# Hardware loops on VectorE and ScalarE in a decode kernel that streams its cache

## The chip, the cores and the metric

The kernel runs on one core of a Trainium2 chip. The metric is the device time of one execution in microseconds (us). A ratio is the mean time of one kernel's runs over the mean of the other's runs of the same rounds, so it is not quite the ratio of the medians that are quoted beside it.

## The reference

One decode step of a block with adaptive layer norm, for 8 sequences of one token each. The attention has 32 query heads over 8 cached key and value heads of 8192 positions and 128 columns each, in bf16. All else is small.

```python
mod = (_silu(c) @ w_mod).reshape(8, 6, 1, -1)
sa, ca, ga, sb, cb, gb = ...                       # six rows of mod
h = _layernorm(x) * (1 + ca) + sa
q = (h @ wq) ...                                   # 8 x 32 heads x 128
scores = einsum('bhqd,bhkd->bhqk', q, k) * 128 ** -0.5
o = einsum('bhqk,bhkd->bhqd', _softmax(scores), v)
x = x + ga * (o @ wo)
h = _layernorm(x) * (1 + cb) + sb
x = x + gb * (relu(h @ w1 + b1) ** 2 @ w2 + b2)
```

Keys and values together are 268 MB. Every byte of them is read once.

## The kernel before

A ring of four slots of 4 MB in SBUF holds "units". A unit is two heads' keys or values of one sequence (called a batch in the code). A batch has four key units and four value units. SyncE issues all loads in order, and each load waits until its slot is released.

The key part of a batch transposes every key tile on TensorE (`key_tiles`). VectorE and ScalarE copy the transposed tiles out of PSUM, and TensorE forms scores. Then come the maximum, the exponentials, and the transposes of the probabilities. In the value part TensorE multiplies each value unit by the probabilities, VectorE copies the sum (`O_sb`), and four small "gather" matmuls bring it into place.

```python
def load(n):                                   # unit n goes to slot n % 4
    ...
    dep = [released.get(s)]
    loaded[n] = dma("sync", s_ring[s], lambda e: e.dma_start(slot(s), src), dep)
...
for b in range(B):
    Pg.at = (b, "a")
    k_Qb = op("vector", lambda e, b=b: e.tensor_copy(Qb[:], QTm[:, b, :, :]), [k_QTm], "vecP")
    for p in range(NP):                        # four key units
        for k in range(4):
            t, toks = key_tiles(n, k, qn % 2)
            if k == 3:
                released[n % NSLOT] = t        # the last key transpose frees the slot
                load(n + NSLOT)
            if pend is not None:
                maxes.append(scores(b, *pend))
    ...                                        # maximum, exponentials
    for k in range(4):
        for i in range(8):
            for hf in range(2):                # two column halves in turn
                t = op("tensor", ... is_transpose=True, tile_position=(0, 64 * hf)) ...
    ...
    for p in range(NP):                        # four value units
        for m in range(32):
            t = op("tensor", ...)              # probabilities times values
        released[n % NSLOT] = t                # the last of them frees the slot
        load(n + NSLOT)
        t = op("vector", ... tensor_copy(osb, Obank) ...)
        for i in range(4):
            t = op("tensor", ... SEL ...)      # the gather
        ... op("vector", ... tensor_tensor(oTn ...))
```

```python
def _tensor(self, eng, passes):
    ...
    with nc.Fori(0, passes, engines=[pe], head_slot={pe: 0}) as i:
        for j, o in enumerate(part((0, "a"))):
            self._emit(eng, o, first["a", j], seen)
        with eng.If(i < passes - 1):
            ...                                # part "b": the values
            self._emit(eng, None, self.per, seen)
            eng.drain()
            for s, n in self.per.items():
                eng.sem_inc(s, -n)
```

## Time and profile before

| | before |
|---|---|
| time, median of 4 | 670.87 us (670.69 to 670.91) |
| read from HBM | 283.66 MB, 424 GB/s over the span |
| data queue's share of 16 DMA engines | 99.0% |
| busy: TensorE, VectorE, ScalarE | 75%, 45%, 35% |

These lines are from the page of the kernel before. The first gives the busy time of the engines in a span of 669.0 us. The DMA and GB/s rows show 40 equal slices, a digit of 9 meaning busy 90% or more. Then come two DMA queues (packets, MB, share of 16 engines): q1 carries the data, q14 instructions. The last two lines give loads by source (count, KB each, median us from issue to landing).

```profile
PE 499.3 (75%) x7348; PEld 340.7 (51%) x7348; DVE 300.2 (45%) x570; ACT 236.1 (35%) x282; POOL 17.5 (3%) x71
...
DMA  9999999999999999999999999999999999999996
GB/s 375 434 405 437 415 435 433 432 427 433 433 437 428 427 437 431 433 429 431 435 435 428 427 433 437 427 429 433 435 437 428 423 435 439 429 427 433 435 410 250
...
q1 hardware_dynamic: 12900, 283.65, 99.0%
...
q14 instruction: 10, 0.07, 0.0%
...
ring<-in_A_k_cache_dram SPq DMA_DIRECT2D x32, 4096.0 KB, 35.1
ring<-in_A_v_cache_dram SPq DMA_DIRECT2D x31, 4096.0 KB, 28.3
```

The DMA is at least 90% busy in every slice but the last. Key loads land 35.1 us (median) after their issue, though one 4 MB unit takes only about 9.7 us (4096 KB at 432 GB/s). So several units are queued at a time. Loads are issued long before their turn.

The windows view of one batch of the kernel before has, per stretch, the length, each engine's busy time with its count, TensorE's granted clock, the DMA share and GB/s. The first stretch is keys and softmax, the second values.

```profile
core 0: us, PE busy (x) PEld busy (x) DVE busy (x) ACT busy (x) POOL busy (x), PEclk, DMA share, GB/s
431.85:480.30 48.45, 47.22 (x726) 35.45 (x727) 32.63 (x57) 28.54 (x34) 0.00 (x0) 0.97 1.00 432
480.30:509.60 29.30, 11.77 (x145) 4.47 (x146) 3.65 (x9) 0.00 (x0) 0.00 (x0) 0.78 1.00 432
```

The stream runs at 432 GB/s in both, although the engines do quite different work in them.

The timeline of the kernel before, around the same batch's turnover, has start, duration, engine, line, operation, tiles, count, and in brackets the idle time before and who ended it.

```profile
474.87 0.69 ACT L533 ACTIVATE P_sb<-PS,negm 128x512 bf16<-128x512 f32 x1 [2.52 <-DVE negm L529]
...
475.70 2.64 PE L542 MATMUL PS<-IDENT,P_sb 128*64 128x128 bf16 x64 [0.15 <-ACT P_sb L533]
...
476.38 2.56 DVE L555 COPY Pm<-PS 64x512 bf16<-64x512 bf16 x6 [1.54 <-PE PS L542]
...
480.29 1.91 PE L583 MATMUL PS<-ring,Pm 128*32 128x512 bf16 x32
482.24 21.60 SPq L344 DMA_DIRECT2D ring<-in_A_k_cache_dram  x4
...
482.99 0.26 PE L596 MATMUL PS<-SEL,O_sb 128*128 128x8 bf16 x4 [0.80 <-DVE O_sb L592]
...
504.64 0.22 DVE L506 COPY Qb<-QTm 128x256 bf16<-128x256 bf16 x1
...
509.58 2.63 PE L451 MATMUL PS<-IDENT,ring 128*128 128x128 bf16 x23 [5.05 <-DMA ring<-in_A_k_cache_dram]
510.65 0.69 DVE L458 COPY KTb<-PS 128x1024 bf16<-128x1024 bf16 x1 [5.79 <-PE PS L451]
511.50 1.02 ACT L456 ACTIVATE KTb<-PS 128x1024 bf16<-128x1024 bf16 x1 [32.52 <-PE PS L451]
```

The last three lines (TensorE, VectorE, ScalarE) show how long the engines wait between batches: TensorE 5.05 us for the DMA, VectorE 5.79 us, ScalarE 32.52 us. The SPq line needs care: it merges four key-load issues, and 21.60 us runs from the start of the first to the end of the last. In narrow windows the trace shows that each takes 0.33 us. The first starts at 482.24, the others are these:

```profile
485.13 0.33 SPq L344 DMA_DIRECT2D ring<-in_A_k_cache_dram  x1
...
493.57 0.33 SPq L344 DMA_DIRECT2D ring<-in_A_k_cache_dram  x1
...
503.51 0.33 SPq L344 DMA_DIRECT2D ring<-in_A_k_cache_dram  x1
```

The value matmuls of the four units end at 482.20, 485.09, 493.52 and 503.46. So each load is issued within 0.05 us of the release of its slot, and none of the four is held up by the DMA. What is queued ahead of a load can be told from the landings in the trace: at 482.24 two value units are outstanding and land at 490.10 and 499.82, 17.6 us later. This is the tightest point of the batch.

### The profile page before, as it was taken

The numbers are of one execution on the slowest core, as the hardware profiler recorded it, in microseconds if no ns is written. First come the engines' busy times: TensorE is split into PE (matmuls) and PEld (weight loads), VectorE is DVE, ScalarE is ACT, GpSimd is POOL, SyncE is SP. The second block draws the span as 40 slices with busy tenths as digits, with TensorE's granted clock in tenths as the row PEclk, the third lists the DMA queues.
The fourth block names the chain that finished last, engine by engine and source line by source line (L and its number), as shares of the span: only waits on it lengthen the run. The fifth ranks groups of instructions, "written<-read, shape, count | busy, mean of one in ns | idle before, by whom it ended". The sixth has DMA issues, their size and how long they took to land.

```text
span 669.0 us, 15914 instructions
## 1 busy us (share of the span) xinstructions
PE 499.3 (75%) x7348; PEld 340.7 (51%) x7348; DVE 300.2 (45%) x570; ACT 236.1 (35%) x282; POOL 17.5 (3%) x71
## 2 busy tenths in 40 slices
PE   3494964899539984699748995399836995489976
PEld 2383731676228751577317751287414772177634
DVE  1262741467216661367315671167513673156722
ACT  2051630466005640266204650066402652046600
POOL 7200000000000000000000000000000000000000
PEclk9696996799859995599968997699977999779985
DMA  9999999999999999999999999999999999999996
GB/s 375 434 405 437 415 435 433 432 427 433 433 437 428 427 437 431 433 429 431 435 435 428 427 433 437 427 429 433 435 437 428 423 435 439 429 427 433 435 410 250
DMA packets 12969, 283.93 MB, mean 424 GB/s; under 512 B 1267, under 2 KB 2324, under 8 KB 4373
## 3 DMA queue, kind: packets, MB, share of 16 engines
q1 hardware_dynamic: 12900, 283.65, 99.0%
q8 instruction: 11, 0.18, 0.1%
q14 instruction: 10, 0.07, 0.0%
q10 hardware_dynamic: 48, 0.02, 0.0%
HBM read 283.66 MB, written 0.01 MB: 424 GB/s over the span
## 4 chain that ended last, share of the span: by engine, by line
PE 50%; DMA 39%; DVE 5%; ACT 2%; SPq 2%; issue 1%
DMA ring<-in_A_k_cache_dram 37%; PE PS L451 36%; PE PS L466 9%; DVE Pm L555 3%; PE PS L583 2%; DMA ring<-in_B_w_dram 2%; SPq L624 2%; ACT KTb L456 1%; ACT P_sb L533 1%; DVE m L471 1%; PE PS L542 1%; PE PS L442 1%; PE PS L562 0%; DVE rhs_r L559 0%; DVE Dm L524 0%
## 5 line engine op out<-in xcount | busy, mean ns | idle before, releaser
L456 ACT ACTIVATE KTb<-PS 128x1024 bf16<-128x1024 bf16 x192 | 196.5, 1024 | 360.2 <-PE PS L451 360.2
L451 PE MATMUL PS<-IDENT,ring 128*128 128x128 bf16 x4096 | 267.6, 228 | 50.7 <-DMA ring<-in_A_k_cache_dram 50.7
L451 PEld LDWEIGHTS PS<-IDENT,ring 128*128 128x128 bf16 x4096 | 246.9, 102 | 99.4 <-DMA ring<-in_A_k_cache_dram 54.0
L458 DVE COPY KTb<-PS 128x1024 bf16<-128x1024 bf16 x320 | 210.1, 687 | 151.1 <-PE PS L451 148.8
L583 PE MATMUL PS<-ring,Pm 128*32 128x512 bf16 x992 | 82.5, 492 | 63.9 <-DMA ring<-in_A_v_cache_dram 63.0
L592 DVE CAST O_sb<-PS 128x512 bf16<-128x512 f32 x31 | 21.4, 692 | 144.5 <-PE PS L583 144.5
L466 PE MATMUL PS<-KTb,Qb 128*32 128x512 bf16 x1024 | 79.2, 386 | 4.5 <-ACT KTb L456 4.5
L583 PEld LDWEIGHTS PS<-ring,Pm 128*32 128x32 bf16 x992 | 29.5, 116 | 102.3 <-DMA ring<-in_A_v_cache_dram 64.4
L442 PE MATMUL PS<-IDENT 128*128 128x512 bf16 x120 | 31.3, 380 | 0.0
L533 ACT ACTIVATE P_sb<-PS,negm 128x512 bf16<-128x512 f32 x32 | 21.5, 685 | 18.9 <-DVE negm L529 18.9
L596 PEld LDWEIGHTS PS<-SEL,O_sb 128*128 128x128 bf16 x124 | 5.3, 99 | 44.8 <-DVE O_sb L592 44.8
L596 PE MATMUL PS<-SEL,O_sb 128*128 128x8 bf16 x124 | 8.0, 171 | 24.8 <-DVE O_sb L592 24.8
L466 PEld LDWEIGHTS PS<-KTb,Qb 128*32 128x32 bf16 x1024 | 15.5, 94 | 21.1 <-ACT KTb L456 8.5
L555 DVE COPY Pm<-PS 64x512 bf16<-64x512 bf16 x48 | 19.5, 419 | 13.4 <-PE PS L542 12.4
L471 DVE TENSOR_REDUCE m<-PS 128x1 f32<-128x512 f32 x32 | 22.0, 689 | 6.6 <-PE PS L466 6.6
L542 PE MATMUL PS<-IDENT,P_sb 128*64 128x128 bf16 x512 | 20.4, 222 | 2.0 <-ACT P_sb L533 1.1
L542 PEld LDWEIGHTS PS<-IDENT,P_sb 128*64 128x64 bf16 x512 | 15.2, 109 | 9.8 <-ACT P_sb L533 9.8
L442 PEld LDWEIGHTS PS<-IDENT 128*128 128x128 bf16 x120 | 9.9, 103 | 10.8 <-issue 3.4
L599 DVE TENSOR_TENSOR oTn<-PS,rinv 128x8 bf16<-128x8 f32 x31 | 6.0, 194 | 10.9 <-PE PS L596 10.9
L377 PE MATMUL PS<-ring,KTb 128*32 128x512 bf16 x56 | 7.2, 627 | 3.7 <-DMA ring<-in_A_wq_dram 3.7
L552 ACT ACTIVATE Pm<-PS 64x512 bf16<-64x512 bf16 x16 | 9.5, 592 | 1.1
L690 ACT ACTIVATE std<-PS,epst 128x8 f32<-128x8 f32 x1 | 0.3, 267 | 25.0 <-PE PS L689 25.0
(126 smaller groups left out, 101.8 us busy)
## 6 DMA issues: line engine op xcount, KB each, us to landing
ring<-in_A_k_cache_dram SPq DMA_DIRECT2D x32, 4096.0 KB, 35.1
ring<-in_A_v_cache_dram SPq DMA_DIRECT2D x31, 4096.0 KB, 28.3
ring<-in_A_wq_dram SPq DMA_DIRECT2D x1, 4096.0 KB, 20.3
ring<-in_w_mod_dram SPq DMA_DIRECT2D x1, 3072.0 KB, 10.4
wo_sb<-in_A_wo_dram SPq DMA_DIRECT2D x1, 3072.0 KB, 45.5
ring<-in_A_v_cache_dram SPq DMA_DIRECT2D x1, 2048.0 KB, 23.4
ring<-in_B_w_dram SPq DMA_DIRECT2D x3, 512.0 KB, 17.6
ring<-in_B_w_dram SPq DMA_DIRECT2D x1, 1344.0 KB, 20.9
```

What stands on the lines that cost most here:

```text
L442: op("tensor", lambda e: e.matmul(bank(at).rearrange("p (a r) -> p a r", a=4), IDENT[:, :], rhs))
L451: t = op("tensor", lambda e, j=j, i=i: e.matmul(STG[j][:, i, :], src[:, 32 * k + 8 * j + i, :], IDENT[:, :], is_transpose=True), [loaded[n ...
L456: stg_free[j] = op("scalar", lambda e, j=j, dst=dst: e.activation(dst, STG[j], ACT.Copy), [t], "scaP")
L458: stg_free[j] = op("vector", lambda e, j=j, dst=dst: e.tensor_copy(dst, STG[j]), [t], "vecP")
L466: t = op("tensor", lambda e, hf=hf, q=q, rhs=rhs: e.matmul(PS[32 * q:32 * (q + 1), k, :], Qb[:, 2 * p + hf, :], rhs, start=(p == 0 and hf ...
L471: return op("vector", lambda e: e.tensor_reduce(m4[:, k:k + 1], bank(k), AX.X, ALU.max), [t])
L533: exps.append(op("scalar", lambda e, k=k: e.activation(P_sb[:, k, :], bank(k), ACT.Exp, bias=negm[:, 0:1], scale=inv_sqrt, accum_out=rs4[: ...
L542: t = op("tensor", lambda e, k=k, i=i, hf=hf, src=src: e.matmul(STG[k][64 * hf:64 * (hf + 1), i, :], src, IDENT[:, :], is_transpose=True, ...
L555: done.append(op("vector", lambda e, dst=dst, frm=frm: e.tensor_copy(dst, frm), [t, k_pm], "vecP"))
L583: t = op("tensor", lambda e, p=p, m=m, cg=cg, vt=vt, Obank=Obank: e.matmul(Obank[32 * cg:32 * (cg + 1), :], lhs[:, p, 32 * m:32 * m + 32], ...
L592: t = op("vector", lambda e, osb=osb, Obank=Obank: e.tensor_copy(osb, Obank), [t], "vecP")
L624: d_w2 = [dma("sync", s_w2[i], lambda e, a=a, z=z, j=j: e.dma_start(W2v[:, a:z, :].rearrange("p (k j) n -> p k (j n)", j=j), B_w2[128 * a: ...
```

## The change

The intent is that VectorE's and ScalarE's instructions also stand only once, in loops like TensorE's. In this code a looped engine takes its own counts off the semaphores at the end of a pass. So there is one semaphore for each pair of engines, and an assertion lets an instruction in the loops signal only one engine. That brings three edits beside the loops. Key slots are released by the next score matmul, since the key transpose already signals a copying engine. Value slots are released by the first gather matmul, which comes after VectorE's copy. The probability transposes go half by half, since each half is copied by an engine of its own.

```diff
+    LOOP = {"tensor": mybir.EngineType.PE, "vector": mybir.EngineType.DVE, "scalar": mybir.EngineType.Activation}
...
+    def index(self, b):
+        return slice(b, b + 1) if self.batch is None else bass.ds(self.batch, 1)
...
+                looped = o.users & set(self.LOOP) if inner(o.at) else set()
+                assert not looped or len(o.users) == 1, (e, o.at, o.users)
+                chan = (e, *looped)
+                if chan not in self.sems:
+                    self.sems[chan] = self.enter(self.nc.semaphore("s_" + "_".join(chan)))
...
-    def _tensor(self, eng, passes):
+    def _looped(self, e, eng, passes):
...
+        with nc.Fori(0, passes, engines=[pe], head_slot={pe: 0} if e == "tensor" else None) as i:
+            self.batch = i
...
-                    if k == 3:
-                        released[n % NSLOT] = t
-                        load(n + NSLOT)
                     if pend is not None:
                         maxes.append(scores(b, *pend))
+                    if k == 3:
+                        released[n % NSLOT] = score_first[0]
+                        load(n + NSLOT)
...
-                for i in range(8):
-                    src = P_sb[:, k, 64 * i:64 * (i + 1)]
-                    for hf in range(2):
+                turned = []
+                for hf in range(2):
+                    for i in range(8):
+                        src = P_sb[:, k, 64 * i:64 * (i + 1)]
                         t = op("tensor", ...)
+                    turned.append(t)
...
-                    released[n % NSLOT] = t
-                    if n + NSLOT < len(units):
-                        load(n + NSLOT)
                     osb = O_sb[:, p % 2, :]
...
+                        if i == 0:
+                            released[n % NSLOT] = t
+                            if n + NSLOT < len(units):
+                                load(n + NSLOT)
...
-                        oTn_p[:, :, p, :, b], ...
+                        oTn_p[:, :, p, :, Pg.index(b)].rearrange("p h r o -> p h (r o)"), ...
```

## The prediction

> **What bounds the kernel now.** A stream out of HBM. The page gives 283.66 MB read in a span of 669.0 us; the data queue takes 99% of what 16 DMA engines have. The windows view of a steady batch shows a DMA share of 1.00 and 432 GB/s both while keys are processed (431.9 to 480.3 us) and while values are (480.3 to 509.6 us). The chain of waits repeats every 78 us, eight 4 MB units at about 9.7 us. TensorE, VectorE and ScalarE are busy 75%, 45% and 35%. Loads are issued far ahead: a median of 35.1 us (keys) and 28.3 us (values) from issue to landing, so about three units are always queued. SyncE's four key-load issues of a batch take 21.6 us together although an unhindered one takes 0.33 us; I read that as a full queue, so those issues wait for the DMA, not for a slot.

> **What the change does.**
> 1. VectorE and ScalarE run eight passes of one loop body (the order of instructions falls from 221 rows to 78 and from 39 to 23). Per pass each pays a wait, a drain, some semaphore decrements and a jump, VectorE also register operations for the batch index. My estimate is 0.5 to 2 us per pass. It falls where both are idle: in the timeline ScalarE has 32.5 us free before a batch's first key copy, VectorE 5.8 us.
> 2. The activation table load moves into the loop: eight loads, 1.28 us each as the trace shows, in ScalarE's 32 us gap. Cost 0.
> 3. A slot is released by the next score matmul (about 0.1 us later), or for values by the first gather matmul, after VectorE's copy: 482.24 to 482.99 us, 0.75 us later. At the tightest point (release of the first value slot) some 17 us of transfers are still queued (my estimate from 9.7 us a unit and landing times). Cost 0.
> 4. Probability transposes go half by half rather than alternating. Sixteen alternating ones took 0.66 us, 41 ns each; full-width key transposes take 59 ns each. [...] if the alternation was overlapping two halves, this is lost: up to 0.3 us per group, 1.2 us per batch, partly repaid because the first half's copy starts earlier. Softmax stretch 9.0 us -> 9 to 10 us. TensorE then waits less for values. Cost 0.
> 5. Fewer instructions are fetched: instruction queues move 0.25 MB, 0.1% of the engines. Gain at most 0.3 us. [...] the new bodies are much shorter than TensorE's, which already loops, so I expect no stall.

> **On the critical path:** almost nothing. Even the tail, where the last weights wait for a value slot, has about 6 us of slack (the first W2 issue blocks for 5.96 us).

> **Prediction:** 670.6 us, range 669.6 to 672.0. Faster by over 2%: 0.01; within 2%: 0.98; slower: 0.01.

> **What would show it right:** DMA share still 99%, 424 GB/s, same 78 us period; TensorE's wait for value DMA falling by about what softmax gains; issue to landing of value-phase loads shorter by 0.5 to 1 us; eight table loads.

> **What would make it wrong:** a loop jump that takes over 6 us beside a saturated DMA, repeated eight times with no slack; the DMA queue running dry at a release; or a later weight issue in the tail, up to 1.5 us.

Items 1 to 4 cost 0 and item 5 gains at most 0.3 us, so 670.87 becomes about 670.6. The loss in item 4 rests on the 41 and 59 ns read from the trace; in item 5 no stall was expected because TensorE loops already.

## The result, and the profile after

The changed kernel takes 670.38 us (median of 4, 669.94 to 670.78) against 670.87 us (670.69 to 670.91). The ratio is 0.9993, with a 95% interval of 0.9976 to 1.001. That is inside the predicted range.

The page of the changed kernel (span 668.9 us), the same lines, with the group of table loads added (count, busy us, mean ns, idle before and its cause):

```profile
PE 501.8 (75%) x7348; PEld 347.5 (52%) x7348; DVE 301.2 (45%) x570; ACT 245.2 (37%) x289; POOL 17.8 (3%) x71
...
DMA  9999999999999999999999999999999999999996
GB/s 373 436 402 435 421 429 435 433 431 427 437 433 433 425 433 435 433 429 429 435 431 435 427 433 435 431 425 433 435 433 431 427 437 433 431 427 433 435 410 246
...
q1 hardware_dynamic: 12900, 283.65, 99.0%
...
q14 instruction: 3, 0.02, 0.0%
...
L472 ACT ACT_TABLE_LOAD x8 | 10.3, 1283 | 3.2 <-issue 3.2
...
ring<-in_A_k_cache_dram SPq DMA_DIRECT2D x32, 4096.0 KB, 33.6
ring<-in_A_v_cache_dram SPq DMA_DIRECT2D x31, 4096.0 KB, 27.8
```

The span, the DMA rows and the rate are as before. The instruction queue q14 carries 3 packets instead of 10. The Exp table is loaded eight times, once per pass. The key loads land 1.5 us sooner after their issue and the value loads 0.5 us sooner, because they are issued later; nothing lands earlier for it.

The windows of the changed kernel, for the same two stretches:

```profile
431.85:479.95 48.10, 47.20 (x725) 35.92 (x722) 32.64 (x57) 29.17 (x35) 0.00 (x0) 0.97 1.01 433
479.95:509.20 29.25, 11.76 (x144) 4.43 (x145) 3.77 (x9) 0.67 (x1) 0.00 (x0) 0.78 1.00 431
```

The stretches are 48.10 and 29.25 us, against 48.45 and 29.30, at 433 and 431 GB/s.

The timeline of the changed kernel at the same turnover:

```profile
474.53 0.69 ACT L554 ACTIVATE P_sb<-PS,negm 128x512 bf16<-128x512 f32 x1 [2.53 <-DVE negm L550]
...
475.36 2.90 PE L564 MATMUL PS<-IDENT,P_sb 128*64 128x128 bf16 x64 [0.15 <-ACT P_sb L554]
...
476.03 2.56 DVE L579 COPY Pm<-PS 64x512 bf16<-64x512 bf16 x6 [1.54 <-PE PS L564]
...
479.34 1.28 ACT L472 ACT_TABLE_LOAD   x1 [0.45 <-issue]
...
479.94 1.91 PE L606 MATMUL PS<-ring,Pm 128*32 128x512 bf16 x32
...
482.86 21.58 SPq L360 DMA_DIRECT2D ring<-in_A_k_cache_dram  x4
...
505.19 0.23 DVE L526 COPY Qb<-QTm 128x256 bf16 x1 [0.70 <-issue]
509.20 2.90 PEld L467 LDWEIGHTS PS<-IDENT,ring 128*128 128x128 bf16 x28 [5.14 <-DMA ring<-in_A_k_cache_dram]
...
510.28 0.69 DVE L474 COPY KTb<-PS 128x1024 bf16<-128x1024 bf16 x1 [4.86 <-PE PS L467]
511.13 1.02 ACT L472 ACTIVATE KTb<-PS 128x1024 bf16<-128x1024 bf16 x1 [30.51 <-PE PS L467]
```

Read against the lines of before:

- The 64 transposes take 2.90 us instead of 2.64. The half-by-half order is slower, as feared: in the records a group of 16 takes 0.89 us instead of 0.64. But from the start of the exponentials to the first value matmul it is 479.94 - 474.53 = 5.41 us, against 480.29 - 474.87 = 5.42 us. VectorE's copies start 1.50 us after the exponentials in this trace and 1.51 us in the other, and last 2.56 us in both. The stretch ends with VectorE's chain, not with the transposes: the copies end at 478.59 (478.94 before), then come the row sums and their reciprocal, which ends at 479.80 (480.14 before), 0.14 or 0.15 us ahead of the value matmul. The transposes are done at 478.26 (478.34 before).
- The key loads are issued at 482.86, right after the first gather matmul instead of the last value matmul. Relative to the first value matmul that is 2.92 us, against 1.95 us before. The four issues again spread over 21.58 us, as the four releases do.
- ScalarE loads its table at 479.34, more than 30 us before its next use.
- VectorE's query copy carries a new idle of 0.70 us: its loop turn. TensorE still waits 5.05 us for the DMA afterwards.

### The profile page after: what moved, and what is told of

Read it like the earlier page. It is cut to its first block, busy times and chain, and to the rows that moved or that the text cites. A ratio compares the mean times of both kernels' runs of the same rounds, so it can differ in the third digit from the quotient of the medians. Undisturbed runs are those within 1.5% of the kernel's fastest.

```text
span 668.9 us, 16042 instructions
## 1 busy us (share of the span) xinstructions
PE 501.8 (75%) x7348; PEld 347.5 (52%) x7348; DVE 301.2 (45%) x570; ACT 245.2 (37%) x289; POOL 17.8 (3%) x71
## 3 DMA queue, kind: packets, MB, share of 16 engines
HBM read 283.66 MB, written 0.01 MB: 424 GB/s over the span
## 4 chain that ended last, share of the span: by engine, by line
PE 54%; DMA 38%; DVE 3%; ACT 2%; SPq 2%; issue 1%
PE PS L467 36%; DMA ring<-in_A_k_cache_dram 36%; PE PS L484 9%; PE PS L564 3%; PE PS L606 2%; DMA ring<-in_B_w_dram 2%; PE PS L458 1%; SPq L648 1%; ACT KTb L472 1%; ACT P_sb L554 1%; DVE m L491 1%; DVE O_sb L612 1%; PE PS L585 0%; DVE Dm L545 0%; PE PS L616 0%
## 5 line engine op out<-in xcount | busy, mean ns | idle before, releaser
L606 PE MATMUL PS<-ring,Pm 128*32 128x512 bf16 x992 | 81.1, 485 | 61.9 <-DMA ring<-in_A_v_cache_dram 61.0
L554 ACT ACTIVATE P_sb<-PS,negm 128x512 bf16<-128x512 f32 x32 | 21.6, 686 | 20.2 <-DVE negm L550 20.2
L564 PEld LDWEIGHTS PS<-IDENT,P_sb 128*64 128x64 bf16 x512 | 21.9, 109 | 5.2 <-ACT P_sb L554 5.2
L564 PE MATMUL PS<-IDENT,P_sb 128*64 128x128 bf16 x512 | 23.2, 222 | 1.2 <-ACT P_sb L554 1.2
L623 DVE TENSOR_TENSOR oTn<-PS,rinv 128x8 f32 (+1 forms) x31 | 6.0, 194 | 14.0 <-PE PS L616 14.0
## 6 DMA issues: line engine op xcount, KB each, us to landing
ring<-in_A_k_cache_dram SPq DMA_DIRECT2D x32, 4096.0 KB, 33.6
```

Of the source, the lines that this page charges most:

```text
L554: exps.append(op("scalar", lambda e, k=k: e.activation(P_sb[:, k, :], bank(k), ACT.Exp, bias=negm[:, 0:1], scale=inv_sqrt, accum_out=rs4[: ...
L564: t = op("tensor", lambda e, k=k, i=i, hf=hf, src=src: e.matmul(STG[k][64 * hf:64 * (hf + 1), i, :], src, IDENT[:, :], is_transpose=True, ...
L606: t = op("tensor", lambda e, p=p, m=m, cg=cg, vt=vt, Obank=Obank: e.matmul(Obank[32 * cg:32 * (cg + 1), :], lhs[:, p, 32 * m:32 * m + 32], ...
```

## The experiments

The theory is that the stream hides everything the change costs. There are two rivals: the costs and gains are real in the chain and cancel out, or the costs are next to nothing even where nothing hides them. Twelve kernels were run. In those called "light" a large part of the cache is not read, so they don't compute the reference; the comparison of outputs evidently doesn't see it.

### straight: the loops alone undone

```diff
-                if e in self.LOOP:
+                if e == "tensor":
                     self._looped(e, eng, passes)
```

> The change without its loops: VectorE and ScalarE unrolled again, the semaphore pairs, the later releases and the half-by-half transposes kept. Theory (the stream of loads hides everything): 670.0 to 671.2 us, one table load of Exp instead of eight, and about ten 8 KB instruction packets instead of three. Rival (loops cost time that some gain elsewhere in the change pays back): the unrolled version is faster than the looped one, by 8 passes of 0.5 us or more, so 666 us or less.

Measured: 670.89 us (670.80 to 671.03) beside 670.77 us for the kernel before, ratio 1.0001 (0.9985 to 1.0018). One table load of Exp, 9 packets on q14. The rival of cancelling gains and losses inside the change is refuted: without the loops there is no gain of 4 us to be found. The step of 0.5 us up to the looped version comes back below.

### light_before, light_after, light_straight: the stream out of the way

Each is its parent with this edit (kernel before, changed kernel, changed kernel unrolled):

```diff
-                loaded[n] = dma("sync", s_ring[s], lambda e: e.dma_start(slot(s), src), dep)
+                w = UNIT if n < 8 else UNIT // 4
+                loaded[n] = dma("sync", s_ring[s], lambda e: e.dma_start(slot(s)[:, 0:w], src[:, 0:w]), dep)
```

> The kernel before with the stream taken out of the way: from the ninth load on only a quarter of each unit is read, the rest of the slot is stale (wrong result on purpose). It should then be bound by the engines. Estimate from the trace of before: 63 us to the first keys as before, then per batch 39 us of keys, 9 us of softmax and 12 us of values, so 8 batches and the tail give about 560 us, DMA share under 50%, hardly any wait of TensorE for DMA after the first batch.

> The changed kernel with the same quarter loads: what the change costs or gains where nothing hides it. Theory A (the costs are there and hidden by the stream): slower than the light version of before by 7 passes of 0.5 to 2 us, 3 to 14 us. Rival B (the costs are next to nothing even unhidden, since VectorE's and ScalarE's jumps fall while TensorE does its own jump and first transposes): within 1.5 us of it.

> Quarter loads, unrolled VectorE and ScalarE, the rest of the change kept. Theory A: equal to the light version of before within 1.5 us and faster than the light looped one by the whole 3 to 14 us, so the loops are the cost. Rival B: all three light versions within 1.5 us. If instead this one is as slow as the light looped one, the transposes' order or the releases are the cost.

Measured: 565.42 us (564.69 to 566.66), 565.75 us (563.53 to 566.23) and 565.00 us (564.35 to 565.28). All three lie within 0.75 us, which is less than the spread of a single one. This is rival B: even with nothing to hide them, the costs of the loops come to nearly nothing. The timelines say why. First the turn from one batch to the next in the light version of before, then in the light changed one:

```profile
424.71 0.25 PE L597 MATMUL PS<-SEL,O_sb 128*128 128x8 bf16 x4 [0.80 <-DVE O_sb L593]
425.00 0.19 DVE L600 TENSOR_TENSOR oTn<-PS,rinv 128x8 bf16<-128x8 f32 x1 [0.35 <-PE PS L597]
425.08 0.22 DVE L507 COPY Qb<-QTm 128x256 bf16<-128x256 bf16 x1
...
426.69 1.50 PE L452 MATMUL PS<-IDENT,ring 128*128 128x128 bf16 x24 [1.73 <-PEq L136]
```

```profile
422.65 0.25 PE L617 MATMUL PS<-SEL,O_sb 128*128 128x8 bf16 x4 [0.80 <-DVE O_sb L613]
...
423.05 0.19 DVE L624 TENSOR_TENSOR oTn<-PS,rinv 128x8 f32 x1 [0.46 <-PE PS L617]
423.95 0.23 DVE L527 COPY Qb<-QTm 128x256 bf16 x1 [0.70 <-issue]
...
424.72 2.50 PE L468 MATMUL PS<-IDENT,ring 128*128 128x128 bf16 x22 [1.81 <-DVE Qb L527]
```

VectorE's turn costs 0.70 us of its time, and ScalarE's about 0.46 us (its seven "issue" waits before the table load sum to 3.2 us in the full-traffic trace). But TensorE makes a turn of its own at the same moment: 1.73 us in the one and 1.81 us in the other between the gather and the first key transpose. VectorE has finished its query copy at 424.18, before TensorE starts at 424.72. What is exposed is at most about 0.1 us a pass, the time by which the indexed multiplication (`oTn`) comes later (idle 0.46 instead of 0.35 us). The batches show not even that: in all three light traces a query copy follows the last after 61.5 to 62.0 us in most batches.

So the stream hides everything, but there was little to hide. What the stream could hide is the next question.

### stall2, stall4, stall6 and light_stall2: how much slack there is

Dummy reductions on VectorE at the end of each of the first seven batches stand in for a slow turn: 2, 4 or 6 of them, on the changed kernel, and 2 on its light version. They measured 4.41 us each. The 4.3 us of the first expectation name no run, but the reductions in the trace of before give about the same: 0.69 us for 128x512 and 0.16 us for 128x4, so about 4.4 us for 128x4096 (an estimate from these two).

```diff
+                    if p == NP - 1:
+                        for x in range(2):     # or 4, or 6
+                            op("vector", lambda e, x=x: e.tensor_reduce(
+                                junk[:, x, :], ONES[:].unsqueeze(1).to_broadcast([128, 32, 128]), AX.X, ALU.max), [k_all])
```

> The changed kernel with two dummy reductions of 128x4096 (estimate 4.3 us each, about 8.6 us) on VectorE at the end of each of the first seven batches, as if its jump back took that long. Theory (slack of the queued loads): VectorE had about 4.9 us free there and some 17 us of transfers are queued, so no change, 670 to 671.5 us, although key processing starts some 4 us late in every batch. Rival (the chain through the engines matters): 7 times 4 us more, about 698 us.

> The same with four reductions, about 17 us. Theory: the keys start some 12 us late, still within the 17 us of queued transfers: 670 to 673 us. Rival: 7 times 12 us more, about 755 us.

> The same with six reductions, about 26 us. Theory: the keys start some 21 us late, 4 us more than the 17 us queued, so the DMA runs dry for 4 us a batch: 690 to 710 us, and the DMA share falls below 97%. Rival without a limit to the slack: still 671 us. Rival with the engines in the chain: about 815 us.

> Control: the two reductions in the version with quarter loads, where no stream hides them. Both theories: VectorE has 1.6 us free there and TensorE can fill some more transposes before it is held up, so 5.5 to 7 us a batch are exposed: 604 to 615 us against 565.75 us without the stall. If it shows nothing, the stall doesn't sit where I think and the ladder proves nothing.

| stall per batch | full traffic | data queue's share | light |
|---|---|---|---|
| none | 670.38 us | 99.0% | 565.75 us |
| 8.8 us | 670.14 us (669.89 to 670.93) | 99.1% | 618.57 us |
| 17.6 us | 680.57 us (679.83 to 681.52) | 98.0% | |
| 26.4 us | 740.13 us (739.70 to 740.57) | 91.7% | |

The control shows that the stall bites where nothing hides it: 52.8 us over seven batches, 7.5 us of the 8.8 (a little more than I expected). With the full stream the same stall costs nothing.

Beyond that my expectations failed. 17.6 us was to be free and cost 10 us; 26.4 us was to cost 20 to 40 us and cost 70. I had added the queued transfers (17 us) to VectorE's idle time (4.9 us) and called the sum the slack. That is the slack for a single delay. A delay that returns in every batch is settled by rates instead. In the trace of the light changed kernel a query copy follows the last after 61.8 us in most batches: that is what the engines need (with a granted clock of 0.945 over that profiled run, against 0.858 in the changed kernel's and 0.846 in stall6's, so for those it is an estimate). The stream needs 77.7 us a batch (query copies at 505.19 and 582.92 us in the changed kernel's trace). The difference is 15.9 us, and about 1.6 us of a stall disappear in VectorE's free time at the turn (8.8 us less the 7.2 us by which the batch of the light stalled version, 69.1 us, is longer). So the limit is about 17.5 us per batch, every batch.

This fits both failed runs. For 26.4 us it gives 61.8 + 26.4 - 1.6 = 86.6 us a batch, and the trace has 85.9 to 87.2 us. For 17.6 us it gives 77.8 us, just at the stream's own period; the later batches of that trace have 78.2 to 78.5 us and its DMA records have no dry gap over 0.3 us before the end. Its 10 us lie in the tail instead. With the stream no longer ahead, TensorE reaches the last units late: the last data come 2.2 us later than in the changed kernel (667.3 against 665.1), and from there to the output's first packet 9.4 us pass, against 2.8 us. This is the timeline of stall4, one turn:

```profile
505.65 17.39 DVE L629 TENSOR_REDUCE junk<-ONES 128x32 f32<-128x4096 f32 x4
...
510.61 3.59 PE L467 MATMUL PS<-IDENT,ring 128*128 128x128 bf16 x32 [5.19 <-DMA ring<-in_A_k_cache_dram]
...
523.73 0.23 DVE L527 COPY Qb<-QTm 128x256 bf16 x1 [0.69 <-issue]
...
524.61 3.60 PE L467 MATMUL PS<-IDENT,ring 128*128 128x128 bf16 x32 [10.40 <-DVE KTb L474]
```

TensorE still waits for the DMA first, 5.19 us. It transposes 32 tiles and then waits 10.40 us more, for VectorE's copy.

### rel_next and rel_last: later releases

```diff
-                            released[n % NSLOT] = t
-                            ...
+   rel_next:               for m in ([n - 1] if p else []) + ([n] if p == NP - 1 else []):
+   rel_last:               for m in [n] if lastb else range(n - 3, n + 1):   # only at p == NP - 1
+                                released[m % NSLOT] = t
+                                ...
```

> The changed kernel with each value slot but the last released one unit later still (by the gather of the next unit): 2.9 us later for the first slot, up to 9.7 us for the others, in place of the 0.75 us of the change. Theory (the release is not what the loads wait for): 670 to 671.5 us, issue to landing of key loads shorter by the delay and their landing times unchanged. Rival (release time is on the chain): each batch longer by 3 us or more, 690 us or more.

> All four value slots of a batch released together by the last gather (the last batch left as it is), to show that the slack is finite. Theory: from the landing of the last value unit the queue is empty until that gather, about 4.5 us, [...]: 6.5 us a batch dry, 7 times that gives 710 to 720 us, with gaps in the DMA once a batch. If the time stays at 671 us, the release plays no part at all and the explanation by slack is wrong.

Measured: rel_next 670.32 us (669.73 to 670.47), ratio 0.9990 (0.9973 to 1.0007). The key loads' issue to landing fell from 33.6 to 24.6 us: issued 9 us later, landed when they would have anyway. So the 0.75 us of the change are far from mattering. rel_last took 719.81 us (719.45 to 720.29). Its DMA records show seven dry gaps of 5.8 to 6.1 us, one per batch, where I expected 6.5 (4.5 us and a term of 2 us: no trace shows it, and in the changed kernel's trace the first data packet starts 1.0 us after the first load's issue, 1.82 against 0.81 us); the period of a batch rose from 77.7 to about 84.8 us. SyncE's part of its timeline:

```profile
539.08 1.85 SPq L360 DMA_DIRECT2D ring<-in_A_k_cache_dram  x4
562.67 29.59 SPq L360 DMA_DIRECT2D ring<-in_A_v_cache_dram  x4
```

Four key-load issues, released together, now take 1.85 us from first to last, not 21.6. So the 21.6 us were the spread of the four releases and not issues held up by a full queue: the loads do wait for their slots. What makes a later release harmless is the 17.6 us of transfers still queued at it. In rel_next the first key load is issued 13.7 us before the unit ahead of it has landed (485.44 and 499.12), and nothing is lost; in rel_last the queue has run dry before the release. The slack of the release is real and finite.

### pool_straight and pool_loop: do instruction packets cost the stream anything?

Three looped kernels had medians of 670.38, 670.14 (stall2) and 670.32 us (rel_next). The unrolled ones had 670.70 to 670.89 us in every set of rounds. No single interval separates them, but the shift is steady: over all sets the 12 looped runs have a mean of 670.29 us and the 38 unrolled ones 670.83. The last two runs asked whether fetching instructions is the reason, by adding 8000 one-element memsets on the idle GpSimd, straight in line or as a loop.

```diff
+                if e == "gpsimd":                                  # pool_straight
+                    for x in [x for _ in range(2) for x in range(4000)]:
+                        if x == 0:
+                            eng.drain()
+                        eng.memset(self.junk[32 * (x % 4):32 * (x % 4) + 1, x // 4:x // 4 + 1], 0.0)
+                if e == "gpsimd":                                  # pool_loop
+                    eng.drain()
+                    with self.nc.Fori(0, 80, engines=[mybir.EngineType.Pool]) as i:
+                        for x in range(100):
+                            eng.memset(...)
+                        eng.drain()
```

> The changed kernel with 8000 one-element memsets on GpSimd, straight in line, after its setup (it is idle then): about 500 KB more instructions, some 60 packets of 8 KB in the instruction queue in place of 3. Question: is the 0.5 us by which the looped versions lie under the unrolled ones real, and is it the instruction packets, each of which holds one DMA engine for 0.3 us? Theory of the packets: 7 packets gave 0.5 us, so 60 more cost 3 to 5 us, 673.5 to 675.5 us. Rival (noise, or something else in the loops): within 0.7 us of the looped control.

> Control: the same 8000 memsets as 80 passes of a hardware loop of 100, so nearly no instruction packets. Both theories: 670.0 to 670.8 us, as the changed kernel. If it is as slow as the straight version, it is the memsets and not the fetching.

As timed runs both failed: 1077.65 and 1108.77 us. I had sized the memsets by the 0.035 us at which the first few of the kernel's own setup follow each other; in these runs one came every 0.13 us, so GpSimd outlasted the kernel and the total says nothing. The traces still answer, since the kernel's own work ends long before. The instruction queue's line of pool_straight, then of pool_loop:

```profile
q14 instruction: 65, 0.53, 0.1%
```

```profile
q14 instruction: 4, 0.03, 0.0%
```

So the straight memsets brought 62 packets and 0.51 MB more than the 3 packets and 0.02 MB of the changed kernel, where I had estimated some 60 and 500 KB. The packets are of 8192 bytes, about one per 129 memsets.

The output is issued at 691.8 us in pool_straight and at 667.5 us in pool_loop (667.1 in the changed kernel). A batch takes 81.0 us in the one and 77.7 us in the other (six batches between query copies: 118.50 to 604.82, and 116.85 to 583.27). The memsets are the same, so it is the fetching. A packet comes about every 16.8 us, some 4.8 in a batch, and the batch is 3.3 us longer: near 0.7 us per packet (an estimate from these numbers).

The landings in the traces agree. In pool_straight, from 110 to 400 us, a unit lands 9.71 to 9.73 us after the one before it when no instruction packet falls between the two, and 10.35 to 10.37 us when one does: 0.65 us per packet. The packet records show where this comes from. Each of the 17 fetches in that stretch took about 0.31 us, and a 32 KB data packet that starts the moment it ends took 1.57 us, where the usual one takes 1.22; together that is 0.66 us. Put end to end by their times, the data packets form 16 chains, one for each DMA engine as I read them (the records don't name the engine). From 110 to 300 us the chain with the fetches finished 150 of them and each other chain 156 or 157, while the total rate, 432 GB/s from 308 to 385 us, was that of pool_loop. As I read it, one engine's share of each such unit came late, and the unit was complete only with that share.

In the kernel before, each of the five instruction packets between 110 and 630 us of the span is followed in the same way by a data packet of 1.59 to 1.88 us. Two of the five, at 364.8 and 517.6 us, show in the landings: those units came after 10.54 and 10.69 us, all others, also those of the other three packets, after 9.70 to 9.73. In the changed kernel there is no instruction packet on this queue there, no 32 KB data packet over 1.3 us, and no unit after more than 9.73 us. So the fetches delay the stream by some 1.8 us in the kernel before and not at all in the changed one. Why only about 0.5 us of this shows in the total is open, and that the fetches are its only cause is not shown.

## Why the prediction was right

- **A stream bounds the kernel.** Right. The full-traffic runs whose queue never ran short (before, changed, straight, stall2, rel_next) all have 424 GB/s and 99% on the data queue, and taking three quarters of the later reads away saved 105 us.
- **SyncE's key-load issues wait for the DMA, not for a slot.** Wrong. The 21.6 us were a merged line; each issue takes 0.33 us and comes within 0.05 us of its slot's release. Nor are three units always queued: at the first value release it is 17.6 us of transfers, less than two units. The forecast did not suffer, since item 3 rests on those 17 us, which came from the landing times.
- **1. The loops' turns cost 0.5 to 2 us where the engines are idle.** Right in kind, at or just under the low end in size: 0.70 us on VectorE, 0.46 us on ScalarE. The reason was too modest. The light runs show that the turns fall beside TensorE's own turn of 1.7 us, so they would be free without the stream too.
- **2. Eight table loads at no cost.** Right: 1.28 us each, at 479.34 in a gap that lasts until 511.13.
- **3. Later releases at no cost.** Right, and by a wide margin (rel_next). The key loads' issue to landing fell by 1.5 us at the median, more than the 0.5 to 1 us forecast, and at the tightest release by 1.0 us (482.24 to 509.53 before, 482.86 to 509.16 after). The two estimates of slack in the text are to be kept apart: "17 us of transfers still queued" is what a single late release may use up, and rel_last shows that this runs out. What a repeated delay may use up is 17.5 us a batch for another reason, engine time against stream time. I mixed the two in the expectations of stall4 and stall6, and both missed.
- **4. The transposes lose overlap.** Right: a group took 0.25 us more, against an estimate of up to 0.3, and the four together 0.26 us, against up to 1.2. In the records of the alternating order the two transposes of a pair start 3 to 4 ns apart, so they did overlap: 16 took 0.64 us alternating and 0.89 us half by half. Only the last of four groups shows its loss, since the exponentials, 0.66 to 0.67 us apart, pace the first three. The softmax stretch stayed at 9.0 us (471.3 to 480.3 before, 471.0 to 479.9 after), so "9 to 10 us" held at its lower end. "TensorE then waits less for values, by about what softmax gains" did not happen as put: the wait went from 63.0 to 61.0 us while softmax gained nothing.
- **5. Instruction fetching gains at most 0.3 us.** This was the mis-sized term. I counted bytes, 0.1% of the traffic. In pool_straight a fetched packet beside the full stream cost a unit 0.65 us, its own 0.31 and 0.35 on the data packet behind it, and the steady shift of the looped kernels is about 0.5 us. The forecast of no stall at the jump was right: the turns took 0.70 and 0.46 us, and the changed kernel's trace has no instruction packet on either queue between about 100 and 640 us.
- **The tail.** Right: the first W2 issue blocked for 5.18 us instead of 5.96, so the slack of about 6 us was used for little.

## What to carry to other kernels

In this kernel, whose stream of loads runs at 432 GB/s and is issued ahead of its turn, an edit to the engines changed the time only when it used up the slack: 8.8 us of stall a batch and the later releases of rel_next cost nothing, 17.6 us of stall cost 10 us, 26.4 us cost 70, and rel_last 49. Such slack can be read in advance: for a delay that returns in every round compare the engines' own time per round with the stream's (here 61.8 and 77.7 us), and for a single delay count the transfers queued at that point (here 17.6 us). Before reading a wait into a merged line of a timeline, ask for its parts. To learn what an edit costs in itself, run both versions with the stream cut down, with a deliberate stall as a control. In this kernel, bound by DMA, looping the engines that are not the bottleneck had one small merit, fewer instruction packets among the data packets. It cost nothing, since their turns (0.70 and 0.46 us) were shorter than TensorE's (1.73 us), beside which they fall.
